# One product instead of two for the maximum over partitions, and a newly worked out order of the instructions

## The chip, the cores and the metric

The kernel runs on one core of one Trainium2 chip. The metric is the device time of one execution in microseconds (us), lower is better. TensorE is written PE (its weight loads PEld), VectorE DVE, ScalarE ACT, GpSimd POOL; SP is the engine whose queue starts the DMAs.

## The reference, cut to what matters

```python
# attention by random features, 4 batches x 8 heads x 576 rows x 64
proj = einsum('bhsd,md->bhsm', x, omega); h = proj - sum(x*x)/2; phi = exp(h - max(h)) / sqrt(m)
kv = einsum('bhsm,bhsd->bhmd', phi(k), v);  z = sum(phi(k))
attn = einsum('bhsm,bhmd->bhsd', phi(q), kv) / (phi(q) . z + 1e-6)
# first gated layer, 2304 tokens, 512 -> 1536 -> 512
xn = attn / rms * rms_g;  y = (silu(xn @ w_gate) * (xn @ w_val)) @ w_out
# second layer, 512 -> 2048 -> 512
out = elu(y @ w_in) @ w_out2
```

The inputs and the output are float32. The kernel keeps float32 accuracy by splitting operands into two float16 halves, high and low, and making three products of them. To split an operand it has to know its largest value: that is where the changed function comes in.

## The kernel before, in words

The 2304 tokens are worked in 9 blocks of 256. The first part of the program is preparation: 20 jobs turn the keys into features (`k_job`, and in it `phi`), 18 do so for the queries and make a 128-token tile of the first layer's input (`q_job`), 12 + 6 loads of weights are split into halves (`conv_cols`, `conv_rows`). The first layer follows per block: six *pairs* (`moe1_pair`: 48 products of 128x128 weights with 256 columns, in two banks of PSUM, then ACT and DVE steps that end in a DVE scalar_tensor_tensor `RM<-RM,ps 128x512`, two per pair), then `moe1_out` (144 products). The second layer follows (`moe2_quad` and `moe2_out`). The products of both layers are called the spine in the code. Preparation of later tiles goes on beside the first layer.

All instructions are recorded as operations with their reads and writes, and a planner (`Plan`) decides, before the program is built, in which order each engine gets them. It steps through its own clock with costs for each operation, and takes, from what is ready on an engine, the operation with the earliest due time. Due times come from the spine (`STRETCH`, `INFL`, `LEAD`) and are shifted per job by `BIAS`. `choose` marks operations that several engines could do; which one gets it follows from the planner's clock and `PRICE` (three numbers for the early part, three for the late one: DVE, ACT, POOL). `BLIM` and `SPARE` limit how many PSUM banks and SBUF slots the preparation may hold. Since everything is issued from one place in the code, all instructions carry the same line, L530; they are told apart by engine, operation and tile. RX, RW, RA, RM, RC, RS, RI and RO are arenas in SBUF (RS: small scalars per partition; RI: the identity `idn` and the vector `ones`; RW: weights; RM and RX: tiles of the layers' inputs), `ps` is PSUM. On every engine instructions start in the order in which they stand.

`spread(m, n)` takes n columns of 128 values, one per partition, and must give each column's maximum in all 128 partitions. Before, a PE product with the column as weight and the identity as moving operand lays the 128 values out along a row of one partition (n rows for n columns), a DVE reduce takes the row's maximum there, and a second PE product, with `ones` as weight, gives that one value to all partitions, in PSUM, from where the consumer reads it. I call the first *product A* (`ps<-RI,RS`, 1x128 or 2x128 in the order) and the second *product B* (`ps<-RS,RI` 128x1, or `ps<-RI` 128x2). There are 52 calls: 44 with n = 1, 6 with n = 2 (the `conv_cols` of the first layer's weights), one with n = 6 and one with n = 8.

Of the kernel before, what the change touches and what calls it, by code (L numbers as in the profile page):

```python
# [12 lines left out]
BF16 = mybir.dt.bfloat16  # L13
AF = mybir.ActivationFunctionType
ALU = mybir.AluOpType
AX = mybir.AxisListType

P = 128
B, S, H, D = 4, 576, 8, 64
# [5 lines left out]
TPE = 1  # L25
KV32 = 2
HALF = 2
AHEAD, BLIM = 2665473.472, 7
QPE = 3
FINE = 9  # L30
BIAS = [0, -24, -6, -13, 9, 11, 1, -18, 4, 16, 26, 0, 3, 0, -42, -66, 48, 0, 24, -36, 11, -47, 60, -76, -82, 71, 3, 7, -74, -72, 7, -40, -68, -29, 214, -138, -2, -19, 6, 12, -10, -26, 30, 98, 29, -5, -6, 50, -58, 0, -29, 29, 0, 7, -28, 113, -9, 8, -23, 3, 1, 0]
LOOK, WEIGH = 0.076, 80
PRICE = [2.61, 1.246, 0.912, 2.233, 0.537, 1.098]
PELEAD = 228143.172
INFL, LEAD = 1.815, 51.617
STRETCH = (11.046, 890.942, 0.188)
NBLK = NT // NB
EXPM = 0x7F800000
SGN = -(1 << 31)
# [100 lines left out]
class Plan:  # L140
# [5 lines left out]
    INTO, FROM = {"POOL": 0.19}, {"PE": 0.22, "POOL": 0.08}  # L146
    LAND, MARGIN = 1.7, 0.5
    SPAN = 3.4133
    SPARE = {"B": 2, "L": 2, "M": 2}
    FIRST = range(38, 57)  # L150

    def __init__(self):
# [152 lines left out]
    def deadlines(self):  # L305
        at = 0.0
        for op in self.ops:
            op.due = 1e9
            if op.spine:
                op.due = at  # L310
                at += op.cost * (STRETCH[0] if at < STRETCH[1] else STRETCH[2])
        for op in reversed(self.ops):
# [3 lines left out]
    def order(self, limit=None):  # L316
        for op in self.ops:
            op.due -= BIAS[op.job] * (not op.spine)
        left = [len(op.deps) for op in self.ops]
# [30 lines left out]
        def gate(op):  # L350
# [10 lines left out]
            for kind, bs in need.items():  # L361
                n, first = len(bs), bs[0].serial == wait[kind][-1].serial
                if len(idle[kind]) < n + (0 if first else self.SPARE[kind]):
                    return None
                xs = [x for x in idle[kind] if x.until > bs[0].first]
                if len(xs) < n + (0 if first else self.SPARE[kind]) or kind == "B" and not first and bs[0].att and held + n > (BLIM if spine else 8):
                    return None
# [8 lines left out]
            if todo and any(w and w[-1].first < op.n and any(x in todo for x in idle[kind])  # L376
                            and sum(x not in todo and x.until > w[-1].first for x in idle[kind]) < self.SPARE[kind] for kind, w in wait.items()):
                return None
# [15 lines left out]

        early, late = [dict(zip(("DVE", "ACT", "POOL"), p)) for p in (PRICE[:3], PRICE[3:])]
        idle = {kind: [x for x in xs if not x.closed] for kind, xs in self.slots.items()}
# [143 lines left out]
def fused(ctx: ExitStack, tc: tile.TileContext, qT, kT, kTt, qn, kn, v, v1, omT, eye, g, wg, wv, wo, w1, w2, out):  # L540
    nc = tc.nc
    plan = Plan()
    vec, act, pool, pe, sp = [plan.engine(n, e) for n, e in (("DVE", nc.vector), ("ACT", nc.scalar), ("POOL", nc.gpsimd), ("PE", nc.tensor), ("SP", nc.sync))]
# [31 lines left out]
    L = [RA.take([1024], F32) for _ in range(7)]  # L575
    M = [RA.take([512], F32) for _ in range(3)]
# [48 lines left out]
    idn, ones, dg = RI.take([P], F16), RI.take([P], F16), RI.take([64], BF16)  # L625
# [5 lines left out]
    def sm(n, name):  # L631
        if (n, name) not in smalls:
            smalls[n, name] = Rot([RS.some([n], F32) for _ in range(6)])
        return smalls[n, name].next()


    def spread(m, n, o=None):

        o = bank.next() if o is None else o
        top = m.bitcast(BF16).rearrange("p (n w) -> p n w", w=2)[:, :, 1]
        pe.matmul(out=o[0:n, 0:P], lhsT=top, rhs=idn, start=True, stop=True)
        if n == 1:
            r = sm(1, "spr").bitcast(BF16)[0:1, 0:1]
            vec.tensor_reduce(out=r, in_=o[0:1, 0:P], op=ALU.max, axis=AX.X)
        else:
            c = sm(1, "spc")
            r = dg[0:n, 0:n]
            vec.tensor_reduce(out=c[0:n], in_=o[0:n, 0:P], op=ALU.max, axis=AX.X)  # L650
            vec.tensor_scalar(out=r, in0=idn[0:n, 0:n], scalar1=c[0:n], scalar2=None, op0=ALU.mult)
        pe.matmul(out=o[:, 504:504 + n], lhsT=ones[0:n], rhs=r, start=True, stop=True)
        return o[:, 504:504 + n]

# [85 lines left out]
    def conv_cols(cv, parts, j, inv):  # L740

        n = len(parts)
        sts = [{} for _ in parts]
        e, s = sm(n, "ce"), sm(n, "cs")
        for i, (st, (w, W)) in enumerate(zip(sts, parts)):
            cv.load(st, src_cols(w, j))
            cv.words(st)
            cv.fp32(st, e[:, i:i + 1])
        plan.serial += 1
        plan.att = False  # L750
        power(e, spread(e, n))
        vec.tensor_scalar(out=inv, in0=e, scalar1=2.0 ** -16, scalar2=2.0 ** -14, op0=ALU.max, op1=ALU.mult)
        vec.reciprocal(out=s, in_=inv)
        for i, (st, (w, W)) in enumerate(zip(sts, parts)):
            cv.split(st, W[:, 0, :, j * 256:(j + 1) * 256], W[:, 1, :, j * 256:(j + 1) * 256], s[:, i:i + 1], n)
# [58 lines left out]
    def row_scales(e, n, ihs, iT, scale, top=14):  # L814

        m = sm(n, "rs")
        plan.serial += 1
        plan.att = False
        power(m, spread(e, n))
        vec.tensor_scalar(out=m, in0=m, scalar1=2.0 ** -16, scalar2=2.0 ** -top, op0=ALU.max, op1=ALU.mult)  # L820
        vec.tensor_tensor(out=m, in0=m, in1=ihs, op=ALU.mult)
        vec.tensor_reduce(out=iT, in_=m, op=ALU.max, axis=AX.X)
        T = sm(1, "T")
        vec.reciprocal(out=T, in_=iT)
        vec.tensor_scalar(out=scale, in0=ihs, scalar1=T, scalar2=None, op0=ALU.mult)
# [16 lines left out]
    def setup_consts():  # L842
        sp.dma_start(out=om[0:64], in_=omT)
        sp.dma_start(out=om2[64:128], in_=omT)
        sp.dma_start(out=idn, in_=eye)
        sp.dma_start(out=gx, in_=g.partition_broadcast(P))
        vec.tensor_scalar(out=om[0:64], in0=om[0:64], scalar1=cc, scalar2=None, op0=ALU.mult)
        vec.memset(om[64:128], -cc * cc / 2.0)
        vec.tensor_scalar(out=om2[64:128], in0=om2[64:128], scalar1=cc, scalar2=None, op0=ALU.mult)
        vec.memset(om2[0:64], -cc * cc / 2.0)  # L850
        vec.memset(mh, -0.5)
        m, m_, mg = sm(1, "m1"), sm(1, "m1b"), sm(1, "mg")
        vec.memset(m, 1e-30)
        vec.tensor_reduce(out=m[0:64], in_=om[0:64], op=ALU.max, axis=AX.X, apply_absolute_value=True)
        vec.memset(ones, 1.0)
        vec.tensor_scalar(out=m_, in0=spread(m, 1), scalar1=1e-30, scalar2=None, op0=ALU.max)
        iw = sm(1, "iw")
        s = pow2(m_, 12, iw)
        for a in (0, 64):
            act.activation(out=Wh[a:a + 64], in_=om[0:64], func=AF.Copy, scale=s[0:64])  # L860
            vec.scalar_tensor_tensor(out=Wl[a:a + 64], in0=om[0:64], scalar=s[0:64], in1=Wh[0:64], op0=ALU.mult, op1=ALU.subtract)
        vec.tensor_copy(out=kap0, in_=iw)
        vec.tensor_reduce(out=mg, in_=gx, op=ALU.max, axis=AX.X, apply_absolute_value=True)
        vec.tensor_scalar(out=mg, in0=mg, scalar1=1e-30, scalar2=None, op0=ALU.max)
        s = pow2(mg, -1, gpow)
        vec.tensor_scalar(out=gx, in0=gx, scalar1=s, scalar2=None, op0=ALU.mult)
# [577 lines left out]
```

## Time and profile before

| | us |
|---|---|
| time, median of 3 runs | 979.05 (977.59 to 979.85) |
| span of the profiled execution | 972.8 |
| PE busy | 911.0 (94%) |
| DVE busy | 667.1 (69%) |
| POOL busy | 599.8 (62%) |
| ACT busy | 537.7 (55%) |

The profile is of one execution and gives its span, from the first instruction to the last; no time of that execution stands beside it. The median of the three timed runs is 6.25 us longer than the span, and the runs lie 4.8 to 7.1 us above it.

### The profile page before, as it was taken

Reading aid. Unit: us, or ns where it says so; the run is one execution under the profiler, and the core shown is the slowest. Engines: PE = TensorE matmul, PEld = TensorE weight load, DVE = VectorE, ACT = ScalarE, POOL = GpSimd, SP = SyncE. Lnnn points to the kernel's source line nnn. Section 1 sums busy time; section 2 is a strip of 40 time slices with the busy share of each in tenths; the row PEclk is TensorE's granted clock in tenths of the full one; section 3 lists DMA queues with packets and bytes.
Section 4 is the critical chain, followed back from the end, with each engine's and each line's share of the span. In section 5 each row is a group of like instructions: output and inputs, shape, how many; then the busy total and the mean of one; then the engine's idle time right before and its main releaser. Section 6 shows DMA issues by size and latency. Waiting matters only on the chain. (4 is left out here: it accounts for less than half of the span.)

```text
span 972.8 us, 22167 instructions
## 1 busy us (share of the span) xinstructions
PE 911.0 (94%) x8904; PEld 802.7 (83%) x8904; DVE 667.1 (69%) x1570; ACT 537.7 (55%) x981; POOL 599.8 (62%) x617
## 2 busy tenths in 40 slices
PE   4486969999999999999999999999999999999998
PEld 4385858888888888888888888888888888888887
DVE  6988887867478585777866888777436565464642
ACT  5895554746455575584533557776435555255540
POOL 3668957967966788688573448996415265153540
PEclk9787989999999999999999999999999999999999
DMA  9765645033511442116674433000000000000001
GB/s 288 209 189 161 173 141 168 7 77 89 131 45 33 88 94 63 37 45 172 196 218 135 142 125 123 31 2 6 18 18 17 12 13 12 17 18 12 12 13 44
DMA packets 82567, 82.57 MB, mean 85 GB/s; under 512 B 52896, under 2 KB 57888, under 8 KB 82464
## 3 DMA queue, kind: packets, MB, share of 16 engines
q1 hardware_dynamic: 82464, 81.16, 29.5%
q8 instruction: 69, 1.13, 0.5%
q14 instruction: 34, 0.28, 0.1%
HBM read 59.90 MB, written 8.91 MB: 71 GB/s over the span
## 5 line engine op out<-in xcount | busy, mean ns | idle before, releaser
L530 PEld LDWEIGHTS <-RW 128*128 128x128 f16 x4800 | 451.7, 98 | 69.0 <-issue 12.2
L530 PE MATMUL ps<-RM,RW 128*128 128x256 f16 (+1 forms) x3240 | 365.4, 271 | 5.0 <-ACT RA L530 3.1
L530 PEld LDWEIGHTS <-RA 128*128 128x128 f16 (+3 forms) x3128 | 261.0, 98 | 31.5 <-issue 1.8
L530 PE MATMUL ps<-RX,RA 128*128 128x256 f16 x1728 | 196.5, 273 | 1.2 <-DVE RM L530 1.2
L530 ACT ACTIVATE RM<-ps,RC 128x512 f32<-128x512 f32 (+1 forms) x135 | 90.0, 669 | 101.7 <-PE ps L530 67.1
L530 POOL TENSOR_TENSOR RA<-RA 64x512 f16<-64x512 f32 (+6 forms) x91 | 122.6, 1349 | 22.8 <-DVE RS L530 4.9
L530 POOL TENSOR_TENSOR RM<-RM 128x512 f16<-128x512 f32 (+1 forms) x94 | 100.9, 1077 | 42.0 <-ACT RM L530 36.2
L530 ACT ACTIVATE RM<-RM 128x512 f32<-128x512 f32 (+3 forms) x163 | 96.3, 592 | 43.9 <-DVE RM L530 39.5
L530 POOL TENSOR_SCALAR RM<-RM,RC 128x512 f32<-128x512 f32 x72 | 57.7, 802 | 93.6 <-ACT RM L530 93.5
L530 DVE SCALAR_TENSOR_TENSOR ps<-ps,RM 128x512 f32<-128x512 f32 x72 | 50.2, 697 | 83.3 <-POOL RM L530 83.3
L530 PE MATMUL ps<-RX,RW 128*128 128x256 f16 x864 | 98.4, 273 | 2.1 <-DMA RX<-RA 2.1
L530 DVE TENSOR_REDUCE RS<-ps 128x4 f32<-128x512 f32 (+5 forms) x146 | 75.4, 536 | 27.6 <-PE ps L530 26.9
L530 DVE SCALAR_TENSOR_TENSOR RM<-RM,ps 128x512 f32<-128x512 f32 x108 | 73.2, 681 | 26.8 <-ACT RM L530 17.9
L530 ACT ACTIVATE RA<-RA 128x1024 f32<-128x1024 f32 (+5 forms) x69 | 61.3, 897 | 49.8 <-DVE RA L530 12.8
L530 PE MATMUL ps<-RW,RA 128*128 128x256 f16 (+2 forms) x560 | 68.5, 276 | 6.1 <-ACT RW L530 4.9
L530 PE MATMUL ps<-RW 128*128 128x256 f16 x600 | 71.9, 273 | 0.9 <-DVE RM L530 0.9
L530 ACT ACTIVATE RA<-RA,RS 64x512 f16<-64x512 f32 (+3 forms) x69 | 51.7, 759 | 27.3 <-POOL RS L530 11.3
L530 POOL TENSOR_TENSOR RW<-RM,RW 128x256 f16<-128x256 f32 (+1 forms) x63 | 43.7, 704 | 34.4 <-ACT RW L530 18.5
L530 POOL TENSOR_SCALAR RA<-RA,RS 64x512 f32<-64x512 f32 (+2 forms) x63 | 43.9, 697 | 22.2 <-ACT RA L530 15.8
L530 POOL TENSOR_TENSOR RA<-RM,RA 128x256 f16<-128x256 f32 (+1 forms) x50 | 34.4, 696 | 32.1 <-ACT RA L530 21.0
L530 DVE SCALAR_TENSOR_TENSOR RM<-ps,RC,RM 128x256 f32<-128x256 f32 x54 | 25.1, 478 | 40.6 <-PE ps L530 40.5
L530 DVE TENSOR_TENSOR RM<-ps,RM 128x256 f32<-128x256 f32 x108 | 45.1, 420 | 9.8 <-ACT RM L530 6.6
(147 smaller groups left out, 1182.4 us busy)
## 6 DMA issues: line engine op xcount, KB each, us to landing
RA<-w SPq DMA_DIRECT2D x32, 512.0 KB, 4.0
RX<-wg SPq DMA_DIRECT2D x12, 512.0 KB, 5.2
RX<-wv SPq DMA_DIRECT2D x12, 512.0 KB, 6.2
RX<-wo SPq DMA_DIRECT2D x12, 512.0 KB, 4.3
out<-RM SPq DMA_DIRECT2D x36, 128.0 KB, 1.7
f<-RA SPq DMA_DIRECT2D x8, 512.0 KB, 3.7
RA<-f SPq DMA_DIRECT2D x8, 512.0 KB, 3.4
RA<-qn SPq DMA_DIRECT2D x11, 256.0 KB, 4.0
```

The source lines that it names most:

```text
L530: getattr(real, fn)(*[fix(x) for x in a], **{i: fix(x) for i, x in k.items()})
```

## The change

`spread` for up to four columns now makes n products whose weight is the column with a step of zero, that is the same column 128 times, and whose moving operand is the identity. Every partition of PSUM then holds all 128 values in a row, and one DVE reduce over rows of 128 gives each partition the maximum, in SBUF. Product B, and for n = 2 a small DVE multiplication between reduce and B, are gone. The two calls with 6 and 8 columns stay as they were. The order is worked out anew with other numbers.

```diff
-AHEAD, BLIM = 2665473.472, 7
+AHEAD, BLIM = 2665473.472, 5
...
-PRICE = [2.61, 1.246, 0.912, 2.233, 0.537, 1.098]
+PRICE = [1.301, 0.231, 0.2, 0.767, 0.205, 0.586]
...
-    SPARE = {"B": 2, "L": 2, "M": 2}
+    SPARE = {"B": 2, "L": 1, "M": 2}
...
         o = bank.next() if o is None else o
         top = m.bitcast(BF16).rearrange("p (n w) -> p n w", w=2)[:, :, 1]
+        if n <= 4:
+            r = sm(n, "spr")
+            with plan.group():
+                for j in range(n):
+                    pe.matmul(out=o[:, j * P:j * P + P], lhsT=top[:, j:j + 1].to_broadcast([P, P]), rhs=idn, start=True, stop=True)
+            vec.tensor_reduce(out=r, in_=o[:, 0:n * P].rearrange("p (n k) -> p n k", n=n), op=ALU.max, axis=AX.X)
+            return r
         pe.matmul(out=o[0:n, 0:P], lhsT=top, rhs=idn, start=True, stop=True)
-        if n == 1:
-            r = sm(1, "spr").bitcast(BF16)[0:1, 0:1]
-            vec.tensor_reduce(out=r, in_=o[0:1, 0:P], op=ALU.max, axis=AX.X)
...
```

`BIAS`, `LOOK`, `INFL`, `LEAD` and `STRETCH` change too; what all these numbers make of the order is seen at three places.

PE early in the program, before: A of one spread and A of another, products of the values' sums (65x128), then B of the second.

```order
L530 LDWEIGHTS RS
L530 MATMUL ps_67<-RI,RS 1x128
L530 LDWEIGHTS RS
L530 MATMUL ps_68<-RI,RS 2x128
L530 MATMUL ps_63<-RW,RA 65x128 x4
L530 MATMUL ps_64<-RW,RA 65x128 x4
L530 LDWEIGHTS RI
L530 MATMUL ps_68<-RI 128x2
```

PE at the same stage of the changed program:

```order
L530 LDWEIGHTS RS
L530 MATMUL ps_67<-RI,RS 128x128
L530 LDWEIGHTS RS
L530 MATMUL ps_67<-RI,RS 128x128
L530 MATMUL ps_68<-RW,RA 65x128 x4
L530 MATMUL ps_61<-RW,RA 65x128 x4
L530 LDWEIGHTS RS
L530 MATMUL ps_62<-RI,RS 128x128
```

The spread with two columns now has two products with 128 rows each, and no B stands behind the products of 65x128.

PE where the first layer has begun, before: the last two-column spread (A), B of a second spread, A and B of a third, then B of the first, and behind them the first layer's products (`RM,RW 128x256`).

```order
L530 LDWEIGHTS RS
L530 MATMUL ps_65<-RI,RS 2x128
L530 LDWEIGHTS RI
L530 MATMUL ps_63<-RS,RI 128x1
L530 LDWEIGHTS RS
L530 MATMUL ps_67<-RI,RS 1x128
L530 LDWEIGHTS RI
L530 MATMUL ps_67<-RS,RI 128x1
L530 LDWEIGHTS RI
L530 MATMUL ps_65<-RI 128x2
L530 LDWEIGHTS RW
L530 MATMUL ps_63<-RM,RW 128x256
```

In the changed program the last two-column spread stands so among the first layer's products:

```order
L530 LDWEIGHTS RW
L530 MATMUL ps_67<-RM,RW 128x256
L530 LDWEIGHTS RS
L530 MATMUL ps_63<-RI,RS 128x128
L530 LDWEIGHTS RS
L530 MATMUL ps_63<-RI,RS 128x128
L530 LDWEIGHTS RW
L530 MATMUL ps_64<-RM,RW 128x256
```

Its maximum goes from DVE to DVE; PE has nothing left to do for it.

DVE in the second layer, before: the merge with the linear part (`ps<-ps,RM 128x512`) waits for a POOL step `RM<-RM,RC 128x512` that stands on POOL.

```order
L530 SCALAR_TENSOR_TENSOR ps_68<-ps_68,RM 128x512
L530 TENSOR_TENSOR RM<-ps_68,RM 128x256
L530 SCALAR_TENSOR_TENSOR RM<-ps_62,RM 128x256
L530 TENSOR_TENSOR RM<-ps_68,RM 128x256
L530 TENSOR_TENSOR RW<-ps_68,RW 128x256 x2
```

DVE in the second layer of the changed program:

```order
L530 TENSOR_TENSOR RM<-RM 128x256
L530 TENSOR_SCALAR RM<-RM,RC 128x512
L530 SCALAR_TENSOR_TENSOR ps_64<-ps_64,RM 128x512
L530 CAST RA<-ps_64 128x256
L530 TENSOR_TENSOR RA<-ps_64,RA 128x256
L530 TENSOR_SCALAR RM<-RM,RC 128x512
L530 SCALAR_TENSOR_TENSOR ps_65<-ps_65,RM 128x512
```

The TENSOR_SCALAR has moved from POOL to DVE for 60 of its 72 instances, and so have 72 subtractions of low halves of 256 columns (RW<-RM,RW, RA<-RM,RA and RM<-RM).

## Rows read from the trace of the kernel before

**Rows 1.** The page: span, busy engines, PE and its clock in 40 slices

```profile
span 972.8 us, 22167 instructions
PE 911.0 (94%) x8904; PEld 802.7 (83%) x8904; DVE 667.1 (69%) x1570; ACT 537.7 (55%) x981; POOL 599.8 (62%) x617
...
PE   4486969999999999999999999999999999999998
...
PEclk9787989999999999999999999999999999999999
```

**Rows 2.** Windows: stretch, its length, busy of each engine (instructions), PE clock, DMA

```profile
0.00:150.00 150.00, 101.91 (x972) 91.22 (x973) 125.97 (x291) 97.28 (x164) 101.95 (x97) 0.86 0.69 198
150.00:600.00 450.00, 444.27 (x4613) 387.11 (x4611) 331.88 (x781) 250.35 (x403) 319.75 (x284) 1.00 0.37 102
600.00:973.00 373.00, 364.86 (x3325) 324.33 (x3322) 209.24 (x498) 190.07 (x416) 178.05 (x238) 1.00 0.06 19
```

**Rows 3.** Waits of PE from 0 to 150: total us, times, longest

```profile
PE ps L530 <- DVE RX L530: 16.5, 2, 12.3
PE ps L530 <- DVE RS L530: 15.0, 7, 6.0
```

**Rows 4.** Chain that ended last: an unbroken run of 256-column products

```profile
836.38 44.71 PE ps L530 x408
```

**Rows 5.** PE's timeline from 552 us: start, us, instruction, count

```profile
552.76 5.41 PE L530 MATMUL ps<-RX,RW 128*128 128x256 f16 x48
558.10 0.22 PE L530 MATMUL ps<-RI,RS 128*1 128x128 f16 x1
558.25 4.10 PE L530 MATMUL ps<-RX,RW 128*128 128x256 f16 x36
562.29 0.17 PE L530 MATMUL ps<-RS,RI 1*128 1x1 bf16 x1
562.39 1.48 PE L530 MATMUL ps<-RX,RW 128*128 128x256 f16 x12
```

**Rows 6.** PE's groups from 150 to 973: products A and B

```profile
L530 PE MATMUL ps<-RI,RS 128*1 128x128 f16 x36 | 7.8, 217 | 2.3 <-DVE RA L530 1.2 <-DVE RS L530 1.0
L530 PE MATMUL ps<-RS,RI 1*128 1x1 bf16 x37 | 6.3, 170 | 1.2 <-DVE RS L530 1.0
```

**Rows 7.** PE's timeline from 95 us: 128-column products with 128-column weights

```profile
95.62 2.17 PE L530 MATMUL ps<-RM,RW 128*128 128x128 f16 x36
97.63 2.00 PE L530 MATMUL ps<-RO,RA 128*128 128x128 f32 x16
```

**Rows 8.** Weight loads by shape: of 128 columns, and of product A

```profile
L530 PEld LDWEIGHTS <-RW 128*128 128x128 f16 x4784 | 451.2, 98 | 69.0 <-issue 12.2 <-DMA RX<-RA 1.6 <-DVE RM L530 1.2
...
L530 PEld LDWEIGHTS <-RS 128*1 128x1 bf16 x44 | 3.4, 79 | 17.1 <-DVE RS L530 9.6 <-issue 3.8 <-DVE RA L530 2.5
```

**Rows 9.** PE's timeline from 137 us, with the wait before a piece in brackets

```profile
137.36 0.22 PE L530 MATMUL ps<-RI,RS 128*1 128x128 f16 x1
143.60 0.16 PE L530 MATMUL ps<-RS,RI 1*128 1x1 bf16 x1 [6.03 <-DVE RS L530]
143.74 0.16 PE L530 MATMUL ps<-RI 2*128 2x2 bf16 x1
143.83 6.44 PE L530 MATMUL ps<-RM,RW 128*128 128x256 f16 x33
```

**Rows 10.** Groups by shape on POOL and DVE: busy us, mean ns, idle before

```profile
L530 POOL TENSOR_SCALAR RM<-RM,RC 128x512 f32<-128x512 f32 x72 | 57.7, 802 | 93.6 <-ACT RM L530 93.5
L530 POOL TENSOR_TENSOR RW<-RM,RW 128x256 f16<-128x256 f32 x60 | 39.8, 674 | 34.4 <-ACT RW L530 18.5 <-DVE RW L530 12.2 <-issue 2.8
L530 DVE TENSOR_TENSOR RM<-ps,RM 128x256 f32<-128x256 f32 x108 | 45.1, 420 | 9.8 <-ACT RM L530 6.6 <-ACT RA L530 0.6 <-ACT RW L530 0.3
L530 DVE TENSOR_REDUCE RS<-ps 1x1 bf16<-1x128 f32 x44 | 12.1, 274 | 9.3 <-PE ps L530 9.2
L530 DVE TENSOR_TENSOR RA<-RA 128x512 f32<-128x512 f32 x10 | 10.9, 1096 | 0.0
L530 DVE TENSOR_SCALAR RA<-RA,RS 128x512 f32<-128x512 f32 x1 | 0.5, 487 | 0.0
```

More of the change, by code (lines that the diff above doesn't have):

```diff
@@ L27 @@
 HALF = 2
-AHEAD, BLIM = 2665473.472, 7
+AHEAD, BLIM = 2665473.472, 5
 QPE = 3
 FINE = 9
-BIAS = [0, -24, -6, -13, 9, 11, 1, -18, 4, 16, 26, 0, 3, 0, -42, -66, 48, 0, 24, -36, 11, -47, 60, -76, -82, 71, 3, 7, -74, -72, 7, -40, -68, -29, 214, -138, -2, -19, 6, 12, -10, -26, 30, 98, 29, -5, -6, 50, -58, 0, -29, 29, 0, 7, -28, 113, -9, 8, -23, 3, 1, 0]
-LOOK, WEIGH = 0.076, 80
-PRICE = [2.61, 1.246, 0.912, 2.233, 0.537, 1.098]
+BIAS = [-1, -24, -8, -11, 9, 12, 1, -21, 3, 17, 38, 13, 13, 7, -32, -122, 58, -23, 26, -47, -6, -101, 80, -618, -107, 41, 2, -32, -361, -77, -42, -74, -11, 24, 213, -74, 15, -997, 5, 12, -13, -27, -10, 1058, 715, -26, -10, 209, -3, 155, -30, 44, 409, 866, 288, 901, 550, 744, 9, 2, -989, -767]
+LOOK, WEIGH = 0.077, 80
+PRICE = [1.301, 0.231, 0.2, 0.767, 0.205, 0.586]
 PELEAD = 228143.172
-INFL, LEAD = 1.815, 51.617
-STRETCH = (11.046, 890.942, 0.188)
+INFL, LEAD = 1.881, 58.265
+STRETCH = (0.286, 0.718, 0.169)
 NBLK = NT // NB
@@ L642, in spread @@
         top = m.bitcast(BF16).rearrange("p (n w) -> p n w", w=2)[:, :, 1]
-        pe.matmul(out=o[0:n, 0:P], lhsT=top, rhs=idn, start=True, stop=True)
-        if n == 1:
-            r = sm(1, "spr").bitcast(BF16)[0:1, 0:1]
-            vec.tensor_reduce(out=r, in_=o[0:1, 0:P], op=ALU.max, axis=AX.X)
[L647 to L651, printed above, removed]
+        if n <= 4:
[5 more added lines that the diff above has]
+            return r
+        pe.matmul(out=o[0:n, 0:P], lhsT=top, rhs=idn, start=True, stop=True)
+        c = sm(1, "spc")
+        r = dg[0:n, 0:n]
+        vec.tensor_reduce(out=c[0:n], in_=o[0:n, 0:P], op=ALU.max, axis=AX.X)
+        vec.tensor_scalar(out=r, in0=idn[0:n, 0:n], scalar1=c[0:n], scalar2=None, op0=ALU.mult)
         pe.matmul(out=o[:, 504:504 + n], lhsT=ones[0:n], rhs=r, start=True, stop=True)
```

## The prediction

> **What bounds the kernel now.** I read the page first. PE is busy for 911.0 of 972.8 us, and its row of 40 slices shows where it is not: the first six slices, some 146 us, are ragged and partly at the lower clock, everything behind is nines at full clock [rows 1]. Cut into three stretches, this becomes plain [rows 2]. From 0 to 150 us PE is busy 101.9 us at a mean granted clock of 0.86, while DVE is busy 126.0 of the 150: here preparation, mostly DVE's, decides. From 150 to 600 PE is busy 444.3 of 450, from 600 to 973 it is busy 364.9 of 373; DVE has 74% and 56% there, POOL 71% and 48%. So behind 150 us the time is the sum of what PE has to do plus 13.9 us, and whatever PE is spared there comes off the end, if its suppliers keep up. In front of 150 us a PE instruction saved is worth nothing by itself; what counts is what PE waits for, and in what order.
>
> PE's waits in that first stretch are led by the first spread's weights, 16.5 us (12.3 of it at the very start, when nothing has been loaded), and by DVE's small results RS, 15.0 us in seven waits [rows 3]. One of the seven is the longest, 6.03 us, and it is a product B: A was issued at 137.36, B could run at 143.60, because DVE had other work queued ahead of the reduce, and PE stood still, with products of the first layer right behind in its queue that ran without a further wait for 6.44 us from 143.83 on [rows 9].
>
> **What a spread costs PE in the full stretch.** An unbroken run of 256-column products takes 44.71 us for 408, that is 0.1096 us each [rows 4]. With it the price of A and B can be read off one spread [rows 5]. 48 products start at 552.76 and should be through the array's front at 558.02; A starts at 558.10 and the next product at 558.25: A costs 0.08 + 0.15 = 0.23 us. 36 products from 558.25 would end at 562.20; B starts at 562.29, the next product at 562.39: 0.09 + 0.10 = 0.19 us. After 150 us there are 36 products A and 37 products B in the records [rows 6], so 36 x 0.23 + 37 x 0.19 = 8.3 + 7.0 = 15.3 us of PE's saturated time is spent on them. Product B also waits, 1.2 us in all there [rows 6].
>
> **What takes their place.** The new product has 128 weight columns and 128 moving columns, with a step of zero in the weight. No row shows a step of zero. Its lower bound is the ordinary product of the same size: 36 of them run from 95.62 to 97.63, 0.056 us each [rows 7]. Its upper bound is A as it is now, 0.23 us, which would mean that A's price has nothing to do with the narrow weight. I take 0.056, because A has the same 128 moving columns as the ordinary product, the same source and the same kind of neighbours, and differs from it in the weight's width alone; the change makes the width that of the ordinary product. The new order has 38 such products after the sixth pair, 2.1 us; at the upper bound they would be 8.7 us. So PE's saturated work falls by 15.3 - 2.1 = 13.2 us, or by 6.6 us at the other end.
>
> [...] The rows say that loading 128 columns takes 98 ns, loading one column 79 ns [rows 8]: nearly the same, and A with the short load is nevertheless dearer in the stream. [...] The measured difference of 19 ns decides here, and 4784 loads of 128 columns already lie beside products.
>
> **DVE's side of a spread.** The reduce of one column read 128 values along a row, 274 ns [rows 10]; now it reads the same 128 values in each of 128 partitions, so the same row prices it, and the consumer's small instruction stays. For two columns a reduce over 256 values takes the place of a reduce and a multiplication; I count that as equal. Nothing is gained or lost in DVE's busy time. What is gained is a crossing from DVE to PE and back within the chain of each scale, and B's place in PE's queue.
>
> **The head.** I take the 6.0 us stall at 137.36 as gone: what stood behind it was ready, and the new order has only products A at that place, whose weight is DVE's input and not its output. The bounds: nothing, if the pairs run out of weights or tiles at the same moment and PE then waits for them instead; and more than that, because DVE's queue has fewer instructions ahead of the same pairs. Ahead of the twelfth pair's last DVE step there were 333 and are 305; 28 instructions at the stretch's mean of 0.433 us (125.97 us for 291) [rows 2] are 12 us. Ahead of the sixth pair the saving is larger, but by the twelfth half of it is given back, so I do not go beyond 12. The queue of SP is reordered as well: the first keys' loads now stand ahead of the first weights', and the first load of the last weight matrix has moved up among the fifth pair of column loads. I price these moves at zero, covered by the same bounds, since PE's two largest waits in this stretch are for DVE and not for a transfer [rows 3].
>
> **Work moved from POOL to DVE.** In the second layer 60 steps of 128x512 go from POOL (802 ns each) to DVE, where the one like instruction took 487 ns; 72 subtractions of 256 columns go over from 674 ns on POOL to something between 420 ns (one operand in PSUM) and half of 1096 ns (both in SBUF, 512 columns); 17 more of 512 columns cost up to 1096 ns [rows 10]. That is 29 + 30 to 39 + 19 us, some 83 us with the middle value, on top of DVE's 209.2 of 373 us: 78%. PE is the busy one there by a margin, and the chain of a quad gets shorter (one crossing and 0.3 us less per bank), so I price the cover at zero for the most part. In the middle stretch ten instructions of 1024 columns and little else come over, 10 us at twice the 487 ns, on 331.9. Because a busier DVE answers later, I add 1 us of new PE waits; if the cover fails, see the rivals.
>
> **The sum.** Span 972.8 - 13.2 (products after 150 us) - 1.2 (waits of B there) - 6.0 (the stall) + 1.0 (DVE) = 953.4. The timed median is 6.25 us above the profiled span, which gives 959.6 us. [...]
>
> **Rivals.** (1) *The zero-step weight is as dear as the narrow one.* Then 6.6 instead of 13.2 us are saved: 966.2. For it: no row shows this operand. Against it: rows 7, as argued. (2) *The head gains as much as DVE's queue shortens*, 12 instead of 6 us: 953.6, and a few us less where a crossing saved shortens the waits that remain. For it: DVE's 84% in the first 150 us. Against: by the thirteenth pair the queues are level again. (3) *Slower: DVE becomes the supplier that PE waits for.* The place is the stretch from 600 us, where conversion of the last weights and the first quads meet: DVE goes from 56% to 78% on average over the whole stretch, and stands higher at its start. Each bank that DVE frees late stops PE, as all engines take their work in order. From 150 us on PE now idles 13.9 us; the change turns slower when this grows by more than 19.4 us, to 33, that is 0.27 us for each of the 72 banks of the second layer. At 0.4 us for each, 29 us, the time would be 988. Against it: DVE's and POOL's sum of work hardly grows, and DVE's step is the faster one. (4) *No gain:* the spared PE time is handed back as waits for preparation in the middle stretch, because DVE's 74% is an average and the same tiles are due earlier; and B's stall reappears as a wait for weights: 977 to 981.
>
> **How the numbers follow.** The forecast has 0.50, with a range of its own from 954 to 966. Rival 1 has 0.14, rival 2 0.14, a half-way loss to waits (967 to 977) 0.07, rival 4 0.05, rival 3 0.10. Faster by over 0.2% (2 us, about what a measurement of this kernel can tell from no change) is 0.50 + 0.14 + 0.14 + 0.07 = 0.85, the same 0.05, slower 0.10. The range from 948 to 971 leaves out rivals 3 and 4 and the worse end of the half-way case.
>
> **What would show it.** In the changed kernel's profile: the new product within the stream of 256-column products, with about 0.06 us between what stands before and behind it (0.23 if rival 1 holds); no group `ps<-RS,RI` any more; the span from 150 us to the end with no more PE idle time than now, 14 us; PE's waits for DVE RS in the first 150 us near 9 instead of 15.0 us; PE running without gaps from about 138 instead of 144 us; POOL's TENSOR_SCALAR `RM<-RM,RC` at 12, DVE's at 60 with about 0.5 us each. The prediction is wrong if PE shows waits for DVE of over 20 us behind 150 us, or if its unbroken stream begins later than at 144 us.

## The result, and the profile after

The changed kernel takes **985.18 us** (median of 7 runs, 980.35 to 986.70) where the kernel before took 977.59 us beside it (7 runs, 974.22 to 979.85): ratio 1.0069, 95% interval [1.0046, 1.0092]. It is slower by 0.7%. The prediction said 959.6 us, 948 to 971, and faster with 0.85.

The page of the changed kernel: span, busy engines, PE and its clock in 40 slices, and the chain that ended last.

```profile
span 983.4 us, 22034 instructions
PE 908.7 (92%) x8860; PEld 809.6 (82%) x8860; DVE 736.6 (75%) x1733; ACT 532.4 (54%) x971; POOL 475.6 (48%) x458
...
PE   5487899799999999999998999899999999999998
...
PEclk9787899899999999999999999999999999999999
...
PE 48%; DVE 23%; DMA 10%; ACT 9%; issue 5%; POOL 5%; SPq 0%; DVEq 0%; ACTq 0%; POOLq 0%
```

A slice is 24.6 us long. Against [rows 1] three slices behind the first six are no longer nines: the ones from 172, from 516 and from 615 us. DVE has 69.5 us more, POOL 124 us less. The chain that ended last has DVE in it for 23%; the chain of before can be followed for 14% of its span only, so the two don't compare. The windows show where the time is lost.

```profile
0.00:150.00 150.00, 110.22 (x995) 99.14 (x996) 112.21 (x256) 97.77 (x160) 99.66 (x98) 0.85 0.67 180
150.00:600.00 450.00, 434.17 (x4569) 387.52 (x4567) 347.21 (x826) 250.37 (x410) 298.69 (x264) 0.99 0.40 108
600.00:700.00 100.00, 89.37 (x795) 77.82 (x793) 89.28 (x188) 63.98 (x133) 42.10 (x49) 0.98 0.06 20
700.00:983.40 283.40, 274.90 (x2510) 245.12 (x2507) 187.87 (x466) 120.29 (x271) 35.10 (x50) 1.00 0.05 17
```

The part of the kernel before from 600 to 700 us, which stood in one row with the rest in [rows 2]:

```profile
600.00:700.00 100.00, 98.46 (x898) 87.21 (x896) 70.22 (x154) 69.04 (x145) 75.30 (x89) 1.00 0.07 24
```

Idle time of PE is the stretch minus its busy time. In the first 150 us it falls from 48.1 to 39.8 us; from 150 to 600 it rises from 5.7 to 15.8; from 600 to 700 from 1.5 to 10.6; from 700 to the end of the span it is 8.5 now and was 6.4 before. Behind 150 us that is 35.0 in place of the prediction's 13.9 us. A marker in the program tells how far the conversion of the last weight matrix is at about 580 us: SP's queue begins there to load the stored matrix again (`RA<-f`). Before and after:

```profile
580.38 17.95 SPq L530 DMA_DIRECT2D RA<-f  x5
```

```profile
581.48 15.31 SPq L530 DMA_DIRECT2D RA<-f  x5
```

PE's own progress can be counted. Behind 600 us it has about 8860 - 995 - 4569 = 3296 products left; the kernel before has 8904 - 972 - 4613 = 3319 [rows 1, rows 2]. The 23 fewer are 2.5 us at 0.1096 us each [rows 4]. So at 600 us the changed kernel is 2.5 us ahead, and this is all that is left of the gain of 20.4 us (13.2 + 1.2 + 6.0) that the prediction had for the products, their waits and the stall. Between 600 and 700 us PE then idles 9.1 us more than before (10.6 - 1.5), while DVE is busy 89.3 of 100 us (70.2 before). PE's waits from 600 us to the end name DVE's and ACT's tiles (total us, times, longest):

```profile
PE ps L530 <- DVE RM L530: 6.8, 7, 1.9
PE ps L530 <- DVE RS L530: 4.3, 1, 4.3
PE ps L530 <- ACT RM L530: 4.1, 3, 1.7
```

The wait for RS is the longest of all, and it stands in front of a new product, the last spread's. At the same place of the kernel before, product A waited 0.98 us, at 620.68:

```profile
621.40 0.23 PE L530 MATMUL ps<-RI,RS 128*128 128x128 f16 x1 [4.35 <-DVE RS L530]
```

The product itself does what was forecast. PE's timeline of the changed kernel from 552 us:

```profile
552.42 0.22 PE L530 MATMUL ps<-RI,RS 128*128 128x128 f16 x1
552.48 2.78 PE L530 MATMUL ps<-RM,RW 128*128 128x256 f16 x24
555.10 2.78 PE L530 MATMUL ps<-RX,RW 128*128 128x256 f16 x24
558.48 0.23 PE L530 MATMUL ps<-RI,RS 128*128 128x128 f16 x1 [0.60 <-DVE RS L530]
558.55 2.78 PE L530 MATMUL ps<-RX,RW 128*128 128x256 f16 x24
```

It starts at 552.42 and its neighbour at 552.48: 0.06 us in the stream, where A and B together took 0.42 [rows 5]. But at 558.48 it stands in front of PE's queue and waits 0.60 us for its weight, which is DVE's result. The groups show both, and the price of DVE's step:

```profile
L530 PE MATMUL ps<-RI,RS 128*128 128x128 f16 x38 | 8.5, 223 | 13.9 <-DVE RS L530 9.1 <-DVE RA L530 2.5 <-DVE RM L530 2.3
```

```profile
L530 DVE TENSOR_SCALAR RM<-RM,RC 128x512 f32<-128x512 f32 x60 | 37.1, 618 | 45.7 <-ACT RM L530 45.6
L530 DVE TENSOR_TENSOR RW<-RM,RW 128x256 f16<-128x256 f32 x29 | 12.7, 452 | 1.1 <-ACT RW L530 1.0
L530 POOL TENSOR_SCALAR RM<-RM,RC 128x512 f32<-128x512 f32 x12 | 10.3, 862 | 23.9 <-ACT RM L530 23.8
```

From 150 us on 38 new products wait 13.9 us in all, where A and B waited 3.5 [rows 6].

### The profile page after: what moved, and what is told of

Read it like the earlier page. It is cut to its first block, busy times and chain, and to the rows that moved or that the text cites. A ratio compares the mean times of both kernels' runs of the same rounds, so it can differ in the third digit from the quotient of the medians.

```text
span 983.4 us, 22034 instructions
## 1 busy us (share of the span) xinstructions
PE 908.7 (92%) x8860; PEld 809.6 (82%) x8860; DVE 736.6 (75%) x1733; ACT 532.4 (54%) x971; POOL 475.6 (48%) x458
## 4 chain that ended last, share of the span: by engine, by line
PE 48%; DVE 23%; DMA 10%; ACT 9%; issue 5%; POOL 5%; SPq 0%; DVEq 0%; ACTq 0%; POOLq 0%
PE ps L530 48%; DVE RM L530 7%; DVE RA L530 5%; DVE RW L530 3%; ACT RA L530 3%; DVE RS L530 3%; DMA f<-RA 3%; ACT RM L530 2%; DVE ps L530 2%; POOL RA L530 2%; ACT RW L530 2%; DMA RX<-wg 2%; DMA RA<-v 2%; DVE RX L530 1%; ACT RX L530 1%
## 5 line engine op out<-in xcount | busy, mean ns | idle before, releaser
L530 PEld LDWEIGHTS <-RW 128*128 128x128 f16 x4816 | 459.1, 99 | 84.0 <-issue 16.0
L530 POOL TENSOR_TENSOR RA<-RA 64x512 f16<-64x512 f32 (+5 forms) x90 | 116.9, 1302 | 40.4 <-DVE RS L530 19.8
L530 POOL TENSOR_TENSOR RM<-RM 128x512 f16<-128x512 f32 (+1 forms) x77 | 82.7, 1082 | 70.9 <-ACT RM L530 65.0
L530 ACT ACTIVATE RA<-RA 128x512 f32<-128x512 f32 (+5 forms) x69 | 62.3, 905 | 54.8 <-DVE RA L530 20.9
L530 ACT ACTIVATE RA<-RA,RS 64x512 f16<-64x512 f32 (+3 forms) x66 | 49.4, 755 | 40.8 <-DVE RS L530 20.4
L530 DVE TENSOR_SCALAR RM<-RM,RC 128x512 f32<-128x512 f32 x60 | 37.1, 618 | 45.7 <-ACT RM L530 45.6
L530 POOL TENSOR_TENSOR RA<-RM,RA 128x256 f16<-128x256 f32 (+1 forms) x22 | 17.8, 814 | 110.5 <-DVE RA L530 58.8
L530 POOL TENSOR_TENSOR RW<-RM,RW 128x256 f16<-128x256 f32 x31 | 21.4, 700 | 98.2 <-ACT RW L530 58.1
L530 PE MATMUL ps<-RW,RA 128*128 128x256 f16 (+2 forms) x544 | 64.5, 273 | 3.6 <-ACT RM L530 2.8
```

Source lines behind the costliest of these rows:

```text
L530: getattr(real, fn)(*[fix(x) for x in a], **{i: fix(x) for i, x in k.items()})
```

## The experiments

Two questions: what does the new product do by itself, and what does the new order do? Each time is compared with the kernel before on the same chip; that one had medians of 976.6 to 978.1 us in these comparisons, so that between experiments of different groups the ratios are the better guide.

**1. The new product in the old order.**

```diff
 # recorded as before (A, reduce, B), then the calls of the same places replaced
+ plan.swap([("matmul", dict(out=o[:, j * P:j * P + P], lhsT=top[:, j:j + 1].to_broadcast([P, P]), rhs=idn, ...)) for j in range(n)])
+ plan.swap([("tensor_reduce", dict(out=R, in_=o[:, 0:n * P].rearrange("p (n k) -> p n k", n=n), ...))], [R])
+ plan.swap([], [R])      # product B's place stays empty
```

> The kernel before with the new spread put in place of the old at the same places: one product per column with the column as a weight of step zero, product B and the small multiplication left out, everything else on every engine in the order and on the engine of before. Theory 1 (the new spread is worth what was predicted, the new order eats it): 13 us of products after 150 us, 1 us of waits of B and up to 6 us of the stall at 137 us come off: 0.980 to 0.986 of before, 958 to 964 us where before takes 977.6. Theory 2 (the new spread itself brings nothing or costs, because its reduce or its zero-step weight is dear): 0.995 to 1.01 of before.

Measured: 973.37 us (971.57 to 975.08, 10 runs), ratio 0.9940 [0.9922, 0.9958], that is 4.8 us faster than before (978.14) and 11.8 faster than the changed kernel. The new product helps, by less than half of the 13.2 us that I had for it behind 150 us. Its windows:

```profile
150.00:600.00 450.00, 432.31 (x4540) 384.76 (x4538) 330.31 (x779) 249.38 (x402) 316.38 (x283) 0.99 0.40 101
600.00:700.00 100.00, 97.40 (x890) 86.54 (x888) 72.81 (x157) 68.63 (x145) 76.34 (x90) 1.00 0.08 26
```

PE's idle time from 150 to 600 us is 17.7 us, 12.0 more than before: in the profiles, what PE is spared stands there as a wait. The reload begins at the same moment as before. That it does so to the hundredth is luck: the profiled execution here, of 975.08 us, is the slowest of the ten, and the one of before was quicker than its median.

```profile
580.38 19.15 SPq L552 DMA_DIRECT2D RA<-f  x5
```

**2. The changed kernel with the old prices of the late part.**

```diff
-PRICE = [1.301, 0.231, 0.2, 0.767, 0.205, 0.586]
+PRICE = [1.301, 0.231, 0.2, 2.233, 0.537, 1.098]
```

> The changed kernel with the last three numbers of PRICE as before, so that in the second layer and its weights' conversion the engines are chosen as before (60 TENSOR_SCALAR and most of the 72 subtractions back on POOL); the first 400 us stay as changed. Theory 1a (VectorE's load from 500 to 700 us makes PE wait): PE's idle time from 600 to 700 us falls from 10.6 to 2 us, and about 10 of the lost us come back: 0.990 times the changed kernel, some 0.997 of before. Rival (that idle time comes from a late end of the preparation and not from the choice of engines): as the changed kernel, 1.007 of before.

Measured: 992.80 us, ratio 1.0138 [1.0104, 1.0171]. Worse, but the planner worked the whole order out again: the reload begins at 597.69, 16 us later than in the changed kernel, so this is another order and not the same one with other engines. It doesn't decide.

**3. Three loads moved ahead in SP's queue.**

```diff
+early = [the first three loads of job 20]
+for op in rest[:wv] + early + rest[wv:]:
```

> The changed kernel with three DMAs moved in SP's queue alone: the three loads of one key job (job 20, third batch) stand ahead of the last gate and output weight loads instead of behind six of them; all other engines' orders are the same. Theory 1b (from 106 to 150 us SP's queue stands behind weight loads that wait for their buffers, and the preparation behind it starves, to make PE wait between 150 and 250 us): 3 to 8 us faster than the changed kernel, 0.999 to 1.004 of before. Rival (the loads of the jobs behind it are late for want of free slots, not for the queue): within 1 us of the changed kernel, 1.007 of before.

Measured: 984.60 us, ratio 1.0058 [1.0038, 1.0077], the changed kernel's own. The place of these loads is not what it waits for.

**4. The last weight's first load held back.**

```diff
+if op.job == 58 and now < 290.0:
+    return None
```

> The changed kernel with the first load of the last weight matrix held back in the planner's clock, so that the SBUF slot that it takes at 68 us stays with the preparation of keys and queries; the order behind it is worked out anew with the same numbers. Theory 1c (that slot is what the preparation lacks between 106 and 150 us): PE's loss between 150 and 250 us, 15 us, shrinks by half or more, 0.999 of before or less. Rival (the slot was not the limit): within 3 us of the changed kernel, 1.004 to 1.010 of before.

Measured: 1086.04 us, ratio 1.1102 [1.1069, 1.1136]. Neither theory's value: the planner's order fell apart, PE was busy 361.35 of the 450 us from 150 to 600. What it was to decide stays undecided; it shows that these order numbers do not carry over to a plan changed at this one place.

**5. PE relieved in the first layer.** From here on only the calls of planned operations are changed, so the order stays. Block 5 of 9 loses 96 products.

```diff
+gemm(pg, cols(WG), j, xa, 4, cut, i == 4)      # and pv: every third product left out
```

> The kernel before with 96 products left out in the first layer (of block 5 of 9, every third product, the low half of the weights; the output loses that part), everything else in place: 96 x 0.1096 = 10.5 us less for PE in the middle of its full stretch. Theory P (what the prediction took for granted: PE's work there adds up to the time): 10.5 us faster, 0.989 of before. Theory S (PE is only as full as its suppliers let it be: the preparation and the conversion of the second layer's weights end when they end, and PE waits for them a little later): 0 to 4 us, 0.996 to 1.000.

Measured: 977.60 us against 976.6, ratio 1.0013 [0.9991, 1.0036]. Nothing of the 10.5 us comes off the time:

```profile
150.00:600.00 450.00, 438.00 (x4514) 378.98 (x4513) 333.54 (x783) 249.91 (x404) 319.24 (x284) 0.99 0.38 102
```

PE's idle time there is 12.0 instead of 5.7 us. The loss can be seen at its place, in the 40 us where the thinned block runs, before and here:

```profile
340.00:380.00 40.00, 39.93 (x424) 34.45 (x422) 32.74 (x88) 26.49 (x51) 33.41 (x36) 1.00 0.38 78
```

```profile
340.00:380.00 40.00, 34.33 (x337) 28.09 (x337) 32.31 (x85) 26.53 (x50) 33.62 (x35) 0.91 0.38 77
```

PE idles 5.6 us more in them, and the granted clock is 0.91 on average where it was 1.00, which is worth another 3.6 us (an estimate: 40 x 0.09). Together that is 9.2 of the 10.5 us. The waits stand in front of the preparation's products and are for DVE's and POOL's results: 1.09 us at 340.83 and 2.36 us at 368.98 for DVE's RS (a product B and a product A), 1.74 us at 348.83 for POOL's RA. PE was busy 99% of the stretch from 150 to 600 us in the kernel before, and yet, at this place, its work did not set the time.

**6. PE relieved in the second layer.**

```diff
+gemm(p, cols(WI), j, ..., 4, thin=i == 6 or i == 7 and m < 2)
```

> The kernel before with 96 products left out in the second layer instead (of the seventh block and half of the eighth, every third product of the first of its two matrices; the output loses that part): the same 10.5 us less for PE, near the end. Theory P: 10.5 us faster, 0.989 of before. Theory S: the same 10 us, since nothing but the second layer's own steps stands against PE there.

Measured: 972.04 us, ratio 0.9956 [0.9941, 0.9971]: 4.6 us less than the 976.6 beside it, of 10.5. Both theories had about 10. Even behind 600 us less than half of what PE is spared comes off the end. From 700 us to the end PE idles 9.2 us, 2.8 more than before; the longest wait, 3.07 us at 891.52 for DVE's RM, was 0.57 us at its place before, and the mean granted clock there is 0.99 instead of 1.00.

**7. The changed kernel with its late steps back on POOL, at the same places.**

```diff
+if op.job in (60, 61) and op.ways and op.eng == "DVE":
+    for w in op.ways:
+        if w.eng == "POOL" and len(w.calls) == 1:
+            op.calls = w.calls
```

> The changed kernel with 161 steps of the second layer and of its weights' conversion moved from VectorE back to GpSimd at the same places in the program (60 TENSOR_SCALAR and 101 subtractions), all else in the same order. Theory D (VectorE at over 90% between 550 and 700 us makes PE wait, and that is what separates the changed kernel from the old order with the new spread): PE's loss from 600 to 700 us falls from 12.8 to 2 to 5 us, 8 to 11 us faster than the changed kernel, 0.996 to 0.999 of before. Rival (the order, not the engine, makes PE wait there): as the changed kernel, 1.005 to 1.009.

Measured: 1001.98 us, ratio 1.0269 [1.0243, 1.0296], slower than the changed kernel, and neither value expected. In this form the theory that DVE's load is the loss is contradicted. From 600 to 700 us DVE is at 50 now, POOL at 80, PE waits more, and its mean granted clock is 0.91:

```profile
600.00:700.00 100.00, 83.92 (x695) 70.99 (x694) 50.03 (x118) 57.01 (x116) 79.74 (x91) 0.91 0.07 25
```

**8. The old order with the new product, most of the last matrix's conversion left out.**

```diff
+if j:
+    for op in plan.ops[n:]: op.calls = []      # and the calls of its other ways
```

> The old order with the new spread, and of the last weight matrix's eight conversions before its store only the first is computed (35 steps on VectorE, ScalarE and GpSimd left out, loads and stores kept; the output is of no use): it takes work from the conversion between 437 and 580 us, none from PE. Theory S: this conversion is the limit against which PE ran when its products became cheaper; with it shortened the new spread shows its worth, 8 us or more faster than the old order with the new spread, 0.986 of before or less. Rival (PE's waits from 400 to 600 us have another cause): within 3 us of the old order with the new spread, 0.992 to 0.996.

Measured: 970.18 us, ratio 0.9933 [0.9910, 0.9956], where experiment 1 has 0.9940 [0.9922, 0.9958]. By the times that is 3.2 us less, by the ratios 0.7, and the intervals overlap, although the reload begins 7.5 us earlier, at 572.89. The conversion isn't the main limit.

**9. The reverse of 7: the old order with the new product, the late steps on DVE.**

```diff
+if op.job in (60, 61) and op.ways and op.eng == "POOL":
+    for w in op.ways:
+        if w.eng == "DVE" and len(w.calls) == 1:
+            op.calls = w.calls
```

> The old issue order with the new partition maxima, and all 248 steps of the late part (the forms of the second layer's weight and the elementwise steps of the second layer) that stood on POOL and may stand on either engine now on DVE, at the same places. Theory D (DVE's load in the late part is what the changed kernel waits for): the changed kernel has the time of these steps on DVE and is 12 us behind the old order with the new maxima (985 against 973), so here the time goes from 973 up to 982 to 988, with DVE over 85 us of 100 busy between 600 and 700 us and PE at 90 or less there. Rival (it isn't the engine but the order in which steps stand): the time stays within 3 us of 973, since DVE's step of 0.62 us is shorter than POOL's.

Measured: 989.84 us (986.35 to 992.35, 6 runs), ratio 1.0122 [1.0093, 1.0151]: 16.5 us more than experiment 1 (18 by the ratios), by the engine of these steps alone, and a little more than the 982 to 988 us expected. The single step is shorter on DVE, 543 ns where POOL took 802 [rows 10], so it is not the step's own length that makes PE wait. The window and PE's timeline (the brackets hold the wait before a piece):

```profile
600.00:700.00 100.00, 87.89 (x775) 76.46 (x774) 90.66 (x216) 62.97 (x130) 0.00 (x0) 0.97 0.07 24
```

```profile
640.95 2.79 PE L552 MATMUL ps<-RX,RA 128*128 128x256 f16 x24 [1.65 <-DVE RM L552]
645.81 1.47 PE L552 MATMUL ps<-RW 128*128 128x256 f16 x12 [2.06 <-ACT RM L552]
665.29 2.78 PE L552 MATMUL ps<-RW 128*128 128x256 f16 x24 [0.98 <-DVE RA L552]
693.30 2.72 PE L552 MATMUL ps<-RW,RM 128*128 128x256 f16 x12 [5.43 <-DVE RM L552]
```

DVE 90.7, PE 87.9: the same picture as in the changed kernel (89.3, 89.4), and the long waits stand in front of products of the second layer. The changed kernel's longest one, in front of the last spread's product, is 1.57 us here.

**10 and 11. The changed kernel with less on DVE in the late part.** In 10 the 32 DVE steps of the second weight's forms and last conversions are left out, in 11 the 60 steps of 618 ns in the second layer's quads.

```diff
+if op.eng == "DVE" and op.job == 60 and op.ways:                                             # 10
+    op.calls = []
+if op.eng == "DVE" and op.job == 61 and op.ways and op.calls[0][1] == "tensor_scalar":       # 11
+    op.calls = []
```

> The changed kernel without the 32 DVE steps of the second weight's forms and last conversions that could stand on either engine (the weight of the second layer is then wrong); everything else stays where it is. They take about 0.4 to 0.8 us each, some 18 us of DVE between 540 and 680 us. Theory D: PE gets back most of what it waits for between 600 and 625 us (4.4 us) and at 650 to 700 us, and the time falls from 985 to 975 to 980. Rival (the order): within 3 us of 985.

> The changed kernel without the 60 DVE steps that scale the exponential in the second layer's quads (0.618 us each, 37.1 us of DVE from 600 us on; the second layer's values are then wrong); everything else stays where it is. Theory D: the time falls from 985 by 6 to 12 us, to 973 to 979, since each quad's chain to PE gets shorter by two such steps and DVE falls under 75 of 100 us between 600 and 700. Rival (the order): within 3 us of 985.

Measured: 10 takes 978.55 us (973.52 to 980.84, 12 runs), ratio 1.0009 [0.9992, 1.0026], 6.6 less than the changed kernel; 11 takes 970.83 us (967.54 to 973.17, 6 runs), ratio 0.9932 [0.9908, 0.9956], 14.4 less (5.9 and 13.4 by the ratios). Both as the theory of DVE's load expects, 11 a little more. Each takes away its own waits. In 10 the wait in front of the last spread's product falls from 4.35 to 0.98 us, and those in front of the second layer's products stay:

```profile
612.14 0.23 PE L530 MATMUL ps<-RI,RS 128*128 128x128 f16 x1 [0.98 <-DVE RS L530]
```

In 11 it is the other way round; of PE's waits behind 600 us the profile names the spread's alone:

```profile
PE ps L530 <- DVE RS L530: 4.2, 1, 4.2
```

A step left out also shortens the chain that it stands in, so 10 and 11 alone don't tell DVE's load from the chain's length; in 9 no step is left out and the moved ones are shorter, and PE waits more. The windows of 11 from 600 us on:

```profile
600.00:700.00 100.00, 95.80 (x867) 85.02 (x865) 84.95 (x185) 67.40 (x142) 46.69 (x54) 0.98 0.07 24
700.00:960.00 260.00, 260.00 (x2384) 232.99 (x2383) 157.50 (x407) 119.94 (x264) 32.61 (x46) 1.00 0.05 17
```

PE's idle time from 600 to 700 us falls from 10.6 to 4.2. DVE's busy share there falls only to 85, not under 75 as I had expected, because the same 100 us now hold more of the layer's work.

**12. The old order with the new product and a lighter preparation.** The edit, in words:

```diff
+if key >= FINE: the calls of the square, of the exponential and of POOL's scaling emptied
```

> The old issue order with the new partition maxima, and in the jobs of keys and queries from the tenth on without three kinds of steps of the preparation that work in place: the square of the raw rows, the exponential, and POOL's scaling of the raw values (the attention's result is then wrong). That is 45 steps less on ACT, about 32 us, and 45 on POOL, about 31 us; PE's work and DVE's are unchanged. Theory S (the preparation's chain sets when PE gets its work until about 580 us): the time falls from 973 by at least 5 us, to 958 to 968, and the load of the stored last matrix, at 580.4 us before and with the new maxima alike, begins earlier by as much. Rival (PE's own work, or DVE's alone, sets the time there): within 2 us of 973.

Measured: 965.46 us (964.44 to 966.51, 5 runs), ratio 0.9877 [0.9855, 0.9900]: 7.9 us less than experiment 1 (6.2 by the ratios), with all of PE's and DVE's work still there. The reload begins 8.9 us earlier, and PE idles 11.7 instead of 17.7 us from 150 to 600. Some of both differences is luck, since the quickest of the five runs was profiled here and the slowest of the ten in experiment 1:

```profile
571.51 24.62 SPq L552 DMA_DIRECT2D RA<-f  x7
```

```profile
150.00:600.00 450.00, 438.28 (x4601) 391.04 (x4601) 337.81 (x793) 235.35 (x381) 296.57 (x246) 0.99 0.41 104
```

## Why the prediction was wrong

**The step that failed** is the first one: "behind 150 us the time is the sum of what PE has to do plus 13.9 us, and whatever PE is spared there comes off the end, if its suppliers keep up". They don't. Taking 10.5 us of products out of the first layer gave nothing: 9.2 of them were lost again at the same place, 5.6 to waits of PE and, by the estimate, 3.6 to a granted clock of 0.91 (5). Taking 28 us from ACT and 31 from POOL in the preparation (their busy time up to 960 us) gave 6 to 8 us (12). And when PE was spared its spreads, the time fell by 4.8 us only (1). This fits a PE and a preparation that the order has matched, PE being just as full as the preparation lets the program go on; it is shown at one block and for one set of preparation steps, not for every part of the stretch. It is also what rival 4 said of the middle stretch, which had 0.05. From 150 to 600 us PE's loads have 86% and its products 99%, both above DVE's 74% [rows 2], and sparing PE work there brought nothing (5).

**The new product's price**, 0.056 us in place of 0.42: right, 0.06 measured. The wider load is hardly longer, as the 98 and 79 ns of [rows 8] had it: the new load takes 100 ns where that of one column takes 79, 21 ns more, and about as long as the ordinary load of 128 columns with its 98. Rival 1 is out. So 13.2 us less of PE's work was about the right size, and the gain from it was the wrong conclusion: the whole kernel with the new product alone gives 4.8 us. Where these 4.8 us come from, the profiles don't show: the two spans are 972.8 and 973.3, the first of an execution quicker than the median, the second of the slowest of ten.

**The head, 6.0 us.** The stall is gone, and the idle time of the first 150 us is 8.3 us smaller. But it is given back at once: PE ran through from 150 to 200 us before, and now stands 6.7 us there; the granted clock, 1.00 before, is 0.93 on average. The windows of before and after, and the two longest waits after:

```profile
150.00:200.00 50.00, 50.00 (x504) 44.29 (x502) 39.26 (x59) 30.04 (x44) 43.79 (x33) 1.00 0.27 71
```

```profile
150.00:200.00 50.00, 43.27 (x415) 37.30 (x413) 46.21 (x90) 31.22 (x49) 35.03 (x24) 0.93 0.40 121
```

```profile
186.46 0.58 PE L530 MATMUL ps<-RA,RX 128*64 128x65 f16 x24 [1.71 <-DVE RM L530]
190.50 0.29 PE L530 MATMUL ps<-RI,RS 128*128 128x128 f16 x1 [3.47 <-DVE RS L530]
```

PE's start without gaps at 138 us, which I had named as a sign, did not come. Its waits for DVE RS in the first 150 us fell below my 9 us, to 0.6, but those for the tiles of weights rose, from 8.4 to 17.4 us for ACT's RW and from 1.0 to 7.0 us for DVE's RW. The new order also has DVE's work later, 13.8 us less of it before 150 us and 7.0 us more from 150 to 200, and a wait for RS stands there now. But the new order is not needed to give the head's gain back. In the old order with the new product (1) PE idles 4.7 us less than before up to 150 us, and then 4.9 us more up to 200, at a granted clock of 0.93 too. It waits 2.28 us for DVE's RM at 141.86 already, and the longest wait is in front of the spread with six columns, for a tile of weights:

```profile
150.00:200.00 50.00, 45.07 (x427) 38.78 (x425) 37.73 (x57) 28.17 (x41) 41.44 (x31) 0.93 0.25 62
```

```profile
167.11 0.27 PE L552 MATMUL ps<-RI,RC 128*6 128x128 f16 x1 [4.08 <-DVE RW L552]
```

The step that failed here is that what stood behind the stall was taken as ready beyond the 6.4 us that [rows 9] show; the prediction had named this case as its lower bound, and rival 4 as a wait for weights.

**POOL to DVE, priced at 1 us.** This term failed as well. It is rival 3, which had 0.10: the conversion of the last weights and the first quads meet behind 600 us and DVE becomes the supplier that PE waits for. The moved steps alone cost 16.5 us in the old order (9), and leaving DVE's steps out gives 6.6 and 14.4 us back in the new one (10, 11). Behind 150 us PE waits 24.9 us for DVE, 6.7 before; over 20 was a sign that the prediction named against itself. My price rested on two things: DVE's average of 78% over 373 us, where the stretch that matters stood at 89%, and a step of 487 ns from a single instruction, which takes 618. That the faster engine takes a step did not help where its queue was the fuller one: in 9 DVE, at 543 ns for a step of 128x512 against POOL's 802, was busy 90.7 of the 100 us from 600 to 700. That the rival's own sum, 988, comes near the measured 985.2 is luck: it had 29 us of new waits behind 600 us on top of a full gain, and the runs have 11.2 us more idle time there (19.1 against 7.9), and hardly any gain.

**The constant of 6.25 us** between span and median was wrong as well. The timed run of the changed kernel with a span of 983.4 us took 985.18, 1.8 us longer than its own span. By this the profiled execution before took some 974.6 us (an estimate), less than any of the three timed runs that I had, and the rest of the 6.25 us is its luck.

**The sum.** The sum had 13.2 + 1.2 + 6.0 - 1.0 = 19.4 us of gain. In the profiled spans, 2.5 us of the first three terms are left at 600 us. Behind 600 us the changed kernel takes 383.4 us and the kernel before 372.8, so with the 2.5 us it loses 13.1 us there. Of these, 9.1 us are idle time of PE from 600 to 700 us and 2.1 us idle time behind 700. Another 1.7 us (an estimate: 10 x 0.17) go to the granted clock, whose mean is 0.83 in the 10 us around the wait of 4.35 us that ended at 621.40; it was 1.00 from 618 to 621.4, 0.57 from 622 to 625, and 1.00 again from 626 to 640:

```profile
618.00:628.00 10.00, 6.59 (x46) 5.30 (x47) 9.80 (x19) 5.66 (x11) 3.19 (x3) 0.83 0.00 0
```

Together these are 12.9 of the 13.1 us. The spans differ by 10.6 us where the medians differ by 7.6, because the profiled execution before was a quick one.

**Open.** Why the late steps put back on POOL at the changed kernel's places (7) are slower still is not shown. PE's waits of 9.6 us there are for DVE's RM, which comes after POOL's step; that POOL's queue of 80 us busy makes it late would fit, and the old order, which has POOL at 76 and DVE at 73 in the same window with PE at 97, is worked out for it. So DVE's load is what PE waits for in both orders with these steps on DVE, but it is not shown that their engine alone makes the changed kernel slower than experiment 1: an order and the engines of its steps go together. No order here takes the new product, is worked out for it, and keeps the late part balanced. Of the kernels here that compute the whole output, experiment 1 is the fastest.

## What to carry to other kernels

A PE that is busy for 99% of a stretch need not be what sets the time there (in 5, 10.5 us of products less were worth nothing): leave a few of its products out, in the order as it is, and see whether the end moves, before any saved product is counted. When an order is worked out anew beside an edit, make the edit in the old order first; here the edit was worth -4.8 us and the order +11.8. And a step moved to a faster engine is priced by that engine's queue in the stretch where the step falls, not by its duration and a mean over the layer: in 9 the moved steps cost 16.5 us.

## What the runs showed of the hardware

A product with a weight of 128 columns that are one column read 128 times goes through PE's stream in 0.06 us, while the product with that one column alone took 0.23 us [rows 5], although its load is shorter; the loads of the two:

```profile
L530 PEld LDWEIGHTS <-RS 128*128 128x128 bf16 x56 | 5.6, 100 | 26.4 <-DVE RS L530 11.4 <-DVE RX L530 10.3 <-DVE RA L530 4.0
```

100 ns here, 79 ns for one column [rows 8]. Taking the weight wider made the product cheaper. This holds at nearly every place behind 200 us where both neighbours are products of 256 columns and nothing waits: from the start of the one neighbour to that of the other, less 0.1096 us, product A costs 0.24 us (24 places), product B 0.20 (23), and the new one 0.055 (24 of 25).

In three stretches in which PE had waited, the mean of the granted clock is below 1.00: 0.83 from 618 to 628 us in the changed kernel (a wait of 4.35 us), 0.91 from 340 to 380 us in experiment 5 (waits of 1.09, 1.74 and 2.36 us), and 0.74 from 687 to 700 us in experiment 9 (a wait of 5.43 us). Behind that last wait 12 products of 256 columns took 2.51 us, from 693.30 to 695.81, that is 0.21 us each in place of 0.1096 [rows 4].

DVE's step of 128x512 that took POOL's place takes 618 ns on average over the 60 in the changed kernel, where POOL is busy 42 of the 100 us from 600 to 700, and 543 ns over 72 in experiment 9, where POOL does nothing there; the one of like shape before had 487 [rows 10]. What makes the difference was not tried:

```profile
L552 DVE TENSOR_SCALAR RM<-RM,RC 128x512 f32<-128x512 f32 x72 | 39.1, 543 | 36.3 <-ACT RM L552 36.0
```
